# Low words of the float64 weights as a bit pattern from ScalarE, joined by one VectorE shift with xor

## The chip, the cores and the metric

The kernel runs on one core of one Trainium2 chip. The metric is the device time of one execution in microseconds (us), the median over runs. Engines are named as in the profile: PE (TensorE), PEld (its weight load), DVE (VectorE), ACT (ScalarE), POOL (GpSimd) and SP (SyncE, which issues most DMAs).

## The reference

Attention in which each query keeps its 32 best scores, and after it a feed-forward layer with a rational function. The feed-forward weights arrive as float64.

```
scores = scale * (q @ k.T)                       # 8 batches, 8 heads, 576 x 576, head_dim 64
kth    = the 32nd largest score of each row
attn   = softmax(where(scores >= kth, scores, -1e9))
x      = (attn @ v), heads side by side          # 4608 x 512
h      = x @ w_in                                # 512 x 2048
g      = (a0 + a1 h + a2 h^2 + a3 h^3) / (1 + |b0||h| + |b1| h^2 + 1e-6)
out    = g @ w_out                               # 2048 x 512
```

## The kernel before

**Attention.** Work goes by tiles of 128 queries of one head: 288 tiles. PE multiplies the scores of a tile into PSUM (`s`, line 583, one buffer of two banks), ACT copies them to `sb` (L590), DVE folds them and takes the best 32 (L609, L615, L626, L634), ACT takes `exp` (L688), DVE multiplies by the mask (L691), PE transposes the result (`trp`, L786), ACT copies that out (L798), and PE multiplies by the values (`av`, L812).

**Feed-forward.** 256 tokens make a chunk, which is complete after 16 tiles. A chunk runs in 8 groups of 256 hidden columns: `ph` (L953) on PE, five or six ACT and POOL steps, and `po` (L1113, L1120) on PE. A weight enters PE as a high part in `float32r` and a low part: `win_h`, `win_l`, and for half of `w_out` a high part in `wout` and a low part that goes to DRAM (`wout_l`) and comes back with each use.

**Weights.** There are 32 blocks of 128x512 (16 of `w_in`, 16 of `w_out`). `weight_block` loads a block's raw 64-bit words in two halves of 256 columns and makes float32 from the two 32-bit words `high` and `low` of each number. Per half: ACT writes the sign (L405); DVE shifts `high` left by three and turns the top bit into a PSUM tile `wb_w` (L412); a second DVE instruction shifts `low` right by 29 and ors it in (L420); ACT takes the absolute value of that (L426); POOL multiplies it by the sign (L430). A split block then gets a high part (L272 on ACT or L274 on POOL, 128x512) and a low part (POOL, L447).

**Order.** The order on every engine is fixed when the kernel is built: each step has a key, and `Plan.run` hands steps to the engines by key, assumed durations and free buffers. `KEY` holds the numbers. Buffers are rings: `t` has 9 tiles of 128x512 for weights and feed-forward, and `mm` has two PSUM banks, which `wb_w`, `trp`, `av` and `ph` share.

Of the kernel before, what the change touches and what calls it, by code (L numbers as in the profile page):

```python
# [12 lines left out]
I32 = mybir.dt.int32  # L13
BF16 = mybir.dt.bfloat16
# [5 lines left out]
KEY = {'LN': 12, 'UV': 'DVE', 'UK': -487.038, 'B0': ('ACT',), 'B1': ('POOL', 'DVE'), 'B2': ('DVE', 'POOL'), 'B3': ('DVE', 'POOL'), 'WH': ('ACT', 'POOL'), 'XH': ('POOL', 'ACT'), 'TH': 0, 'EU': -7.115, 'HW': 256, 'Q0': ('POOL', 'ACT'), 'Q1': ('POOL',), 'SPLIT': (0, 2, 4, 6), 'XS': 1, 'RH': ('ACT',), 'p2': ('POOL',), 'p4': ('POOL',), 'ratio': ('POOL',), 'ratio_low': ('POOL',), 'URG': -136.228, 'PT': -6.247, 'AV': -10.804, 'MOE': 55.899, 'LOOK': 0.277, 'T': 5.777, 'KL': 0.63, 'PJ': 40.462, 'WL': -6.889, 'EX': 42.775, 'EW': 13.493, 'ALT': {'ACT': 0.085, 'DVE': 78.296, 'POOL': 1.153}, 'WG': 0.783, 'QL': -3.371, 'PACE': 11.084, 'WI': 0, 'WO': 0, 'MS': -0.081, 'NM': ('POOL',), 'WD': ('POOL', 'ACT'), 'LP': ('POOL',), 'VL': -12.627}  # L20
# [157 lines left out]
def tile_topk_attention__then__rational_ffn(  # L178
# [10 lines left out]
    nc = tc.nc  # L189
# [19 lines left out]
    C1 = 1.0 + 1e-6  # L209
    HW = KEY['HW']  # L210
# [71 lines left out]
    def small(engs, long=0):  # L282
# [25 lines left out]
    nc.vector.tensor_scalar(far, far, 1.0 / 64.0, 1e-10, op0=ALU.mult, op1=ALU.add)  # L308
    tiny = const.tile([P, 1], F32, name="tiny")
    nc.gpsimd.memset(tiny, 1e-9)  # L310

    win_h = const.tile([P, HP, DFF], F32R, name="win_h")
    win_l = const.tile([P, HP, DFF], F32R, name="win_l")
    wout = [
        const.tile([P, DM], F32R if f // FG in SPLIT else F32, name=f"wout{f}") for f in range(NF)
    ]
# [12 lines left out]
    def weight_block(src, r0, e0, split, tags, key, nm, bits):  # L329
# [3 lines left out]
        steps = []  # L333
        hi, lo, away = split
        plain = lo is None and away is None
        hold = [Hold(n, 2 if plain and f64 else 1) for n in tags]
        xhold = Hold("mm", 2)

        def words(i, dtype=F32):
            n = hold[min(i, len(hold) - 1)]  # L340
            if n.tag != "xs":
                return buf(n, [P, 512], dtype, f"w_{nm}_{i}")
            if i % 2 == 0:
                o.big = buf(n, [P, HP, NT], dtype, f"w_{nm}_{i}", "hl"[i // 2])
                o.big = o.big.rearrange("p c n -> p (c n)")
            return o.big[:, (i % 2) * 512 : (i % 2 + 1) * 512]

        if not f64:

            def load():  # L350
                o.w = hi if plain else words(0)
                o.low = words(3 if f64 else 1, F32R) if away is not None else lo
                nc.sync.dma_start(o.w, rows)

            hold = [] if plain else hold[0 : 1 if away is None else 2]
            last = [add("SP", dma(1, P * 512), load, key=key, take=hold)]
        else:

            def load():
                o.raw, o.plain = [], []  # L360
                for i, e in enumerate(range(0, 512, 256)):
                    r = words(i).bitcast(I32)
                    nc.sync.dma_start(r, rows[:, e : e + 256].bitcast(I32))
                    o.plain.append(r.bitcast(F32)[:, 0:256])
                    r = r.rearrange("p (e t) -> p e t", t=2)
                    o.raw.append((slice(e, e + 256), r[:, :, 0], r[:, :, 1]))
                o.w = hi if plain else words(2)
                o.low = words(3, F32R) if away is not None else lo

            ld = add("SP", dma(2, P * 1024), load, key=key, take=hold)  # L370
            last, first = [], []
            for i in range(2):


                def upper(i=i):
                    es, low, high = o.raw[i]
                    nc.vector.tensor_scalar(
                        o.w[:, es].bitcast(I32), high, 3, 0x3FFFFFF8,
                        op0=ALU.logical_shift_left, op1=ALU.bitwise_and,
                    )  # L380

                def lower(i=i):
                    es, low, high = o.raw[i]
                    x = o.w[:, es].bitcast(I32)
# [4 lines left out]
                def ends(i=i):  # L389
                    es, low, high = o.raw[i]  # L390
                    x = o.w[:, es].bitcast(I32)
                    nc.vector.scalar_tensor_tensor(
                        x, high, -0x40000000, x, op0=ALU.bitwise_and, op1=ALU.bitwise_or
                    )

                if bits:
                    s1 = add("DVE", 0.38, upper, [ld], key + 1)
                    s2 = add("DVE", 0.5, lower, [s1], key + 1)
                    last.append(add("DVE", 0.5, ends, [s2], key + 2, give=hold if plain else []))
                    continue  # L400


                def sign(i=i):
                    es, low, high = o.raw[i]
                    nc.scalar.activation(o.w[:, es], high.bitcast(F32), AF.Sign)  # L405


                def high(i=i):
                    es, low, high = o.raw[i]
                    if i == 0:  # L410
                        o.bits = bank(xhold, [P, 512], f"wb_{nm}").bitcast(I32)
                    nc.vector.tensor_scalar(  # L412
                        o.bits[:, es], high, 3, 0x40000000,
                        op0=ALU.logical_shift_left, op1=ALU.bitwise_xor,
                    )

                def low(i=i):
                    es, low, high = o.raw[i]
                    x = o.bits[:, es]
                    nc.vector.scalar_tensor_tensor(  # L420
                        x, low, 29, x, op0=ALU.logical_shift_right, op1=ALU.bitwise_or
                    )

                def size(i=i):
                    es, low, high = o.raw[i]
                    nc.scalar.activation(o.plain[i], o.bits[:, es].bitcast(F32), AF.Abs)  # L426

                def join(i=i):
                    es, low, high = o.raw[i]
                    nc.gpsimd.tensor_tensor(  # L430
                        out=o.w[:, es], in0=o.plain[i], in1=o.w[:, es], op=ALU.mult
                    )

                s1 = add("ACT", act_sb(256), sign, [ld], key + 1)
                s2 = add("DVE", dve(256), high, [ld] + first, key + 1, take=[] if first else [xhold])
                first = [s2]
                s3 = add("DVE", dve(256), low, [s2], key + 1)
                s4 = add("ACT", act(256), size, [s1, s3], key + 2, give=[xhold])
                last.append(
                    add("POOL", pool_t(256), join, [s4], key + 2, give=hold if plain else [])  # L440
                )

        def high_part():
            affine(hi, o.w, 1.0, 0.0)

        def low_part():
            engine().tensor_tensor(out=o.low, in0=o.w, in1=hi.bitcast(F32), op=ALU.subtract)  # L447
# [8 lines left out]
        return [  # L456
            add("SP", dma(1, P * 512), lambda: nc.sync.dma_start(away, o.low.bitcast(F32)), [s],
                key + 3, give=hold)
        ]

    w_steps = {}

    def add_weights(key0, gap):
        n = 0
        blocks = []
        for e in range(0, DFF, 512):
            for c in range(HP):
                split = (win_h[:, c, e : e + 512], win_l[:, c, e : e + 512], None)
                tags = ["xs"] if c == HP - 1 and e < DFF // 2 else ["t"] * 3
                blocks.append((("i", c, e // 512), w_in, c * P, e, split, tags))  # L470
            for f in range(4 * (e // 512), 4 * (e // 512) + 4):
                split = (wout[f], None, wout_l.get(f))
                tags = ["t"] * (4 if f // FG in SPLIT else 2)
                blocks.append((("o", f), w_out, f * P, 0, split, tags))
        for n, (name, *args) in enumerate(blocks):
            bits = name[2] >= 4 - KEY["WI"] if name[0] == "i" else name[1] >= 16 - KEY["WO"]
            w_steps[name] = weight_block(*args, key0 + n * gap, f"w{n}", bits)
# [462 lines left out]
    def add_group(x, o, g, key, split, xs, oholds):  # L940
# [6 lines left out]
        def hidden(f, c):  # L947
            def emit():
                if f == 0 and c == 0:
                    y.ph = bank("mm", [P, 512], f"ph_{nm}")  # L950
                fs = slice((g * FG + f) * P, (g * FG + f + 1) * P)
                for i, (w, z) in enumerate(((win_h, o.xh), (win_h, o.xl), (win_l, o.xh))):
                    nc.tensor.matmul(  # L953
                        y.ph[:, f * NT : (f + 1) * NT], w[:, c, fs], z[:, c, :],
# [385 lines left out]
```

## Time and profile before

| what | value |
|---|---|
| median of 3 runs (lowest, highest) | 1576.05 us (1574.21, 1578.91) |
| the profiled execution's own time | 1577.03 us |
| its span, first to last instruction | 1574.9 us |
| mean granted TensorE clock | 0.967 of full |

2.1 us of the profiled execution lie outside its span. Busy time of an engine is the time in which it had an instruction; instructions of one engine overlap by some tenths of a microsecond, so means of single instructions add up to more than it.

### The profile page before, as it was taken

How to read it: one execution, taken by the hardware profiler on the slowest of the kernel's cores; microseconds unless marked ns; L12 is line 12 of the kernel's file. 1: busy time of each engine (PE TensorE's matmuls, PEld its weight loads, DVE VectorE, ACT ScalarE, POOL GpSimd, SP SyncE). 2: the span in 40 equal slices, each digit the busy share in tenths (PEclk: the TensorE clock that was granted, in tenths of full speed). 3: DMA queues.
4: the chain of work that ended last, by engine and by line, in shares of the span. 5: the costliest groups of instructions: out<-in, count | busy, mean ns of one | idle time of the engine just before them, and what ended most of it. 6: DMA issues, size and time to landing. Idle time of an engine off the chain costs nothing.

```text
span 1574.9 us, 31365 instructions
## 1 busy us (share of the span) xinstructions
PE 1436.9 (91%) x9441; PEld 1120.1 (71%) x9441; DVE 1415.8 (90%) x5605; ACT 1332.3 (85%) x2487; POOL 1144.2 (73%) x1601
## 2 busy tenths in 40 slices
PE   2346998988999899999999999999999999999996
PEld 1234776757777777777777877787787778788774
DVE  6998999999999999499999999999999999799742
ACT  5666897969898898899989998999897988798863
POOL 7767785758866796869867886678787896788520
PEclk9756999999999999999999999999999999999998
DMA  7544234122422233223432234224322333121111
GB/s 226 187 154 156 80 96 130 52 77 71 138 83 70 79 109 113 68 66 88 123 95 80 76 118 119 72 58 123 121 75 72 96 100 98 52 70 50 48 48 49
DMA packets 86802, 148.93 MB, mean 95 GB/s; under 512 B 12640, under 2 KB 38240, under 8 KB 86624
## 3 DMA queue, kind: packets, MB, share of 16 engines
q1 hardware_dynamic: 86560, 146.83, 31.4%
q8 instruction: 77, 1.26, 0.3%
q14 instruction: 101, 0.83, 0.2%
q0 software_dynamic: 64, 0.00, 0.1%
HBM read 134.22 MB, written 12.58 MB: 93 GB/s over the span
## 4 chain that ended last, share of the span: by engine, by line
PE 67%; POOL 8%; DVE 7%; ACT 6%; issue 2%; DMA 1%; POOLq 0%; ACTq 0%; DVEq 0%; SPq 0%
PE ph_m L953 18%; PE po_m L1113 11%; PE po_m L1120 9%; PE av L812 9%; PE s L583 7%; PE trp L786 6%; PE ph_t L953 3%; DVE m L626 2%; PE po_t L1113 1%; DVE pr L609 1%; PE s L580 1%; PE po_t L1120 1%; POOL pa_m L1041 1%; DVE pr L691 1%; ACT e L688 1%
## 5 line engine op out<-in xcount | busy, mean ns | idle before, releaser
L953 PE MATMUL ph_m<-xh_m,win_h 128*128 128x256 f32 x1024 | 316.4, 309 | 9.2 <-ACT p L798 8.8
L626 DVE MAX8 m<-x 128x8 f32<-128x192 f32 (+1 forms) x864 | 308.9, 358 | 3.6
L953 PE MATMUL ph_m<-xl_m,win_h 128*128 128x256 f32 x1024 | 289.5, 283 | 1.0 <-POOL xl_m L916 1.0
L953 PE MATMUL ph_m<-xh_m,win_l 128*128 128x256 f32 x1024 | 289.5, 283 | 0.0
L786 PE MATMUL trp<-ident,pr 128*128 128x128 f32 x1312 | 223.3, 281 | 45.0 <-DVE pr L691 24.3
L798 ACT COPY p<-trp 128x512 f32<-128x512 f32 (+1 forms) x448 | 230.2, 518 | 38.6 <-PE trp L786 25.4
L583 PE MATMUL s<-k,q 128*128 128x288 f32 x1024 | 209.5, 328 | 55.6 <-DVE x L609 36.4
L1113 PE MATMUL po_m<-wout,pa_m 128*128 128x512 f32 x512 | 248.2, 594 | 0.0
L786 PEld LDWEIGHTS trp<-ident,pr 128*128 128x128 f32 x1312 | 162.1, 144 | 109.2 <-issue 28.1
L609 DVE TENSOR_TENSOR pr<-s,sb 128x192 f32<-128x192 f32 x576 | 198.4, 346 | 41.7 <-PE trp L786 30.1
L688 ACT ACTIVATE e<-sb,st 128x576 f32<-128x576 f32 x288 | 218.7, 759 | 18.4 <-POOL st L280 11.5
L691 DVE SCALAR_TENSOR_TENSOR pr<-sb,m,e 128x576 f32<-128x576 f32 x288 | 230.3, 800 | 2.0 <-DVE x L615 0.2
L590 ACT COPY sb<-s 128x576 f32<-128x576 f32 x288 | 186.4, 647 | 51.8 <-PE s L583 45.0
L583 PEld LDWEIGHTS s<-k,q 128*128 128x128 f32 x1024 | 154.9, 196 | 98.3 <-ACT w_w L426 21.6
L953 PEld LDWEIGHTS ph_m<-xh_m,win_h 128*128 128x128 f32 x1024 | 195.2, 191 | 26.2 <-ACT p L798 13.9
L953 PEld LDWEIGHTS ph_m<-xl_m,win_h 128*128 128x128 f32 x1024 | 195.8, 191 | 8.3 <-issue 5.7
L615 DVE MAX8 x<-pr 128x8 f32<-128x192 f32 x576 | 199.1, 346 | 0.2
L634 DVE MATCH_REPLACE8 x<-m,x 128x192 f32<-128x192 f32 x576 | 198.0, 344 | 0.1
L953 PEld LDWEIGHTS ph_m<-xh_m,win_l 128*128 128x128 f32 x1024 | 195.1, 191 | 0.0
L812 PE MATMUL av<-p,vm 128*64 128x256 f32 (+1 forms) x1920 | 186.7, 343 | 2.6 <-ACT p L798 2.5
L812 PEld LDWEIGHTS av<-p,vm 128*64 128x64 f32 x1920 | 111.5, 142 | 82.9 <-issue 14.6
L975 POOL TENSOR_TENSOR pa_m<-pa_m,hh_m 128x512 f32<-128x512 f32 x88 | 113.2, 1286 | 38.6 <-ACT pa_m L972 38.0
(131 smaller groups left out, 3588.5 us busy)
## 6 DMA issues: line engine op xcount, KB each, us to landing
wl_m<-wout_l SPq DMA_DIRECT2D x128, 256.0 KB, 2.7
vm<-in_v_dram SPq DMA_DIRECT2D x96, 320.0 KB, 2.9
kx<-in_qk_dram SPq DMA_DIRECT2D x32, 576.0 KB, 3.9
qx<-in_qk_dram SPq DMA_DIRECT2D x64, 256.0 KB, 2.9
km<-in_qk_dram SPq DMA_DIRECT2D x32, 352.0 KB, 3.3
w_w<-in_moe_w_in_dram SPq DMA_DIRECT2D x32, 256.0 KB, 4.3
w_w<-in_moe_w_out_dram SPq DMA_DIRECT2D x32, 256.0 KB, 3.4
out_dram<-ob_m SPq DMA_DIRECT2D x64, 128.0 KB, 1.7
```

The costliest lines, as they stand in the source:

```text
L583: nc.tensor.matmul(s[:, hf, 0:HF], u.pair.q.q[:, i, t.h, o : o + P], kv.k[:, t.h, cols], start=(i == 0), stop=(i == 1),)
L609: engine().tensor_tensor(out=to, in0=one_, in1=two_, op=op)
L615: nc.vector.max(t.x[:, o : o + 8], t.w[:, 2 * i * TH :][:, 0:TH])
L626: nc.vector.max(t.m[:, 8 * r : 8 * r + 8], src)
L634: nc.vector.match_replace(y, t.m[:, 8 * r : 8 * r + 8], x, NEG)
L688: nc.scalar.activation(t.e, t.sb, AF.Exp, scale=SCALE, bias=t.st)
L691: nc.vector.scalar_tensor_tensor(out=t.pr, in0=t.sb, scalar=t.kth, in1=t.e, op0=ALU.is_ge, op1=ALU.mult, accum_out=u.ss[:, t.h : t.h + 1],)
L786: nc.tensor.transpose(u.ps[i][:, c * P : (c + 1) * P], u.pr[:, x], ident)
L798: nc.scalar.copy(pair.pT[i][:, at].rearrange("p c n -> p (c n)"), u.ps[i][:, 0 : n * P])
L812: nc.tensor.matmul(pair.av[d, 0 : u.nq * len(pair.units)], lhs, x[:, 0, d] if u.mixed else x[:, 0] if lone else x, start=(c == 0), stop=(c ...
L953: nc.tensor.matmul(y.ph[:, f * NT : (f + 1) * NT], w[:, c, fs], z[:, c, :], start=(c == 0 and i == 0), stop=(c == HP - 1 and i == 2),)
L1113: nc.tensor.matmul(o.po[i], y.pa[:, at], wout[ff], start=(ff == 0), stop=(ff == NF - 1),)
```

## The change

Per half block the work is divided anew. ACT reads `low` as an unsigned integer, multiplies it by 0.936 times two to the minus 51 and adds 2.0 (bias from a tile `two`); the float32 result has the bit pattern 0x40000000 with the wanted three bits at its end, and goes to PSUM. One DVE instruction shifts `high` left by three and xors it in. ACT then takes the sign of `high` in place, and the absolute value of the PSUM tile; POOL multiplies. `w_in` blocks load their raw words into the places of `win_h` and `win_l` (now 16 tiles each), so that only the float32 block takes a `t` tile; a `w_out` block takes two `t` tiles where a split one took four, its parts are made in them, and the high part is copied to `wout` by a further instruction (`high_again`). At most two `w_out` blocks are under way (`wt`).

Some 20 numbers in `KEY` change. The key step from one weight block to the next (`WG`) goes from 0.783 to 4.177, where a tile's step is 5.8 in both; the high parts may now go to POOL first (`WH`). `HW`, `SPLIT` and the shapes of all other instructions are as before.

```diff
@@ weight_block
-                def high(i=i):
-                    es, low, high = o.raw[i]
-                    if i == 0:
-                        o.bits = bank(xhold, [P, 512], f"wb_{nm}").bitcast(I32)
-                    nc.vector.tensor_scalar(
-                        o.bits[:, es], high, 3, 0x40000000,
-                        op0=ALU.logical_shift_left, op1=ALU.bitwise_xor,
-                    )
-
-                def low(i=i):
-                    es, low, high = o.raw[i]
-                    x = o.bits[:, es]
-                    nc.vector.scalar_tensor_tensor(
-                        x, low, 29, x, op0=ALU.logical_shift_right, op1=ALU.bitwise_or
-                    )
...
+                def low(i=i):
+                    es, low, high = o.parts[i]
+                    if i == 0:
+                        o.bits = bank(xhold, [P, 512], f"wb_{nm}")
+                        o.w = words(0) if lo is not None else hi if plain else hi(F32)
+                    nc.scalar.activation(o.bits[:, es], low.bitcast(U32), AF.Identity, scale=STEP, bias=two_)
+
+                def high(i=i):
+                    es, low, high = o.parts[i]
+                    x = o.bits[:, es].bitcast(I32)
+                    nc.vector.scalar_tensor_tensor(
+                        x, high, 3, x, op0=ALU.logical_shift_left, op1=ALU.bitwise_xor
+                    )
...
+                s1 = add("ACT", act(256), low, [ld] + first, key + 1,
+                         take=[] if first else [xhold] + (hold if lo is not None else []))
+                first = [s1]
+                s2 = add("DVE", dve(256), high, [s1], key + 1)
+                s3 = add("ACT", act_sb(256), sign, [s2], key + 1)
+                s4 = add("ACT", act(256), size, [s2], key + 2, give=[xhold])
                 last.append(
-                    add("POOL", pool_t(256), join, [s4], key + 2, give=hold if plain else [])
+                    add("POOL", pool_t(256), join, [s3, s4], key + 2, give=hold[i : i + 1] + turn[0 : i] if plain else [])
                 )
...
+        if f64:
+            steps.append(add(one(512, 0, KEY['WH']), None, high_again, [s], key + 3, give=hold[0:1]))
+        return steps
```

In the changed kernel the lines are: L390 `low`, L395 `high`, L401 `sign`, L405 `size`, L409 `join`, L274 or L276 the high parts, L431 the low part, L577 the copy to `sb`.

The first place is DVE between the best-of-eight steps of the first tile (`x`, `m`, `pr` are the tile's buffers, `wb_w` the bank of a weight block, `w_w` raw words). Before:

```order
L634 MATCH_REPLACE x_0_0_181<-m_0_0_201,x_0_0_181 128x192
L412 TENSOR_SCALAR wb_w_214<-w_w_0_144 128x256
L626 MAX m_0_0_201<-x_0_0_181 128x8
L420 SCALAR_TENSOR_TENSOR wb_w_214<-w_w_0_144,wb_w_214 128x256
L634 MATCH_REPLACE x_0_0_181<-m_0_0_201,x_0_0_181 128x192
L412 TENSOR_SCALAR wb_w_214<-w_w_1_146 128x256
L626 MAX m_0_0_201<-x_0_0_181 128x8
L420 SCALAR_TENSOR_TENSOR wb_w_214<-w_w_1_146,wb_w_214 128x256
```

The same place in the changed kernel:

```order
L621 MATCH_REPLACE x_0_0_174<-m_0_0_191,x_0_0_174 128x192
L395 SCALAR_TENSOR_TENSOR wb_w_194<-win_h_0_142,wb_w_194 128x256
L613 MAX m_0_0_191<-x_0_0_174 128x8
L596 TENSOR_TENSOR pr_0_0_173<-s_0_0_1_184,sb_0_0_1_200 128x192
L621 MATCH_REPLACE x_0_0_174<-m_0_0_191,x_0_0_174 128x192
L596 TENSOR_TENSOR pr_0_0_173<-s_0_0_1_184,sb_0_0_1_200 128x192
L596 TENSOR_TENSOR pr_0_0_173<-s_0_0_1_184,pr_0_0_173 128x192
L613 MAX m_0_0_191<-x_0_0_174 128x8
```

Where four weight instructions stood between the tile's steps, one stands now, and folds of the next tile have moved up.

The second place is the start of ACT. Before:

```order
L405 ACTIVATE w_w_2_132<-w_w_0_128 128x256
L405 ACTIVATE w_w_2_132<-w_w_1_130 128x256
L426 ACTIVATE w_w_0_128<-wb_w_150 128x256
L426 ACTIVATE w_w_1_130<-wb_w_150 128x256
L405 ACTIVATE w_w_2_140<-w_w_0_136 128x256
L405 ACTIVATE w_w_2_140<-w_w_1_138 128x256
L295 ACTIVATE co<-co 128x2
L590 COPY sb_0_0_0_174<-s_0_0_0_163 128x576
L426 ACTIVATE w_w_0_136<-wb_w_169 128x256
```

In the changed kernel, from the second weight block on:

```order
L390 ACTIVATE wb_w_156<-win_h_0_127,two 128x256
L390 ACTIVATE wb_w_156<-win_l_0_128,two 128x256
L577 COPY sb_0_0_0_162<-s_0_0_0_151 128x576
L401 ACTIVATE win_h_0_127<-win_h_0_127 128x256
L401 ACTIVATE win_l_0_128<-win_l_0_128 128x256
L405 ACTIVATE w_w_0_157<-wb_w_156 128x256 x2
L390 ACTIVATE wb_w_194<-win_h_0_142,two 128x256
L577 COPY sb_0_0_1_200<-s_0_0_1_184 128x576
L390 ACTIVATE wb_w_194<-win_l_0_143,two 128x256
```

ACT now opens a block's bank (L390) as well as closing it (L405), and the copies of score tiles stand inside that stretch; from its first to its last ACT instruction a block spans 3.4 rows of ACT before and 13.1 now, mean of the first 27 blocks.

The third place is ACT in the first feed-forward groups (`hh_m`, `pa_m`, `va_m`, `h_m`, `g_m` are the steps of a group). Before:

```order
L965 ACTIVATE hh_m_0_1_1751<-ph_m_0_1_1665 128x512
L272 ACTIVATE g_m_0_0_1758<-pa_m_0_0_1638 128x512
L798 COPY p_0_4_3_1762<-trp_0_4_3_1754 128x256
L972 ACTIVATE pa_m_0_1_1772<-ph_m_0_1_1665,co 128x512
L590 COPY sb_3_0_0_1780<-s_3_0_0_1764 128x576
L1023 ACTIVATE va_m_0_1_1790<-ph_m_0_1_1665 128x512
```

In the changed kernel, a few rows later in the same groups:

```order
L274 ACTIVATE g_m_0_0_1797<-pa_m_0_0_1605 128x512
L980 ACTIVATE va_m_0_1_1760<-va_m_0_1_1760,co 128x512
L390 ACTIVATE wb_w_1821<-w_w_0_1539,two 128x256
L577 COPY sb_3_0_1_1830<-s_3_0_1_1805 128x576
L390 ACTIVATE wb_w_1821<-w_w_1_1540,two 128x256
L274 ACTIVATE q_2_2_1843<-qx_2_2_1258 128x512
L401 ACTIVATE w_w_0_1539<-w_w_0_1539 128x256
L401 ACTIVATE w_w_1_1540<-w_w_1_1540 128x256
L405 ACTIVATE wout_1822<-wb_w_1821 128x256 x2
```

Before, no weight instruction stands behind the first group; now five of the 32 blocks do.

## Rows read from the trace of the kernel before

**Rows 1.** The page: span, busy time of the engines, PE and DVE in 40 slices.

```profile
span 1574.9 us, 31365 instructions
...
PE 1436.9 (91%) x9441; PEld 1120.1 (71%) x9441; DVE 1415.8 (90%) x5605; ACT 1332.3 (85%) x2487; POOL 1144.2 (73%) x1601
...
PE   2346998988999899999999999999999999999996
...
DVE  6998999999999999499999999999999999799742
```

**Rows 2.** Windows: start:end, length, busy us of each engine, granted PE clock, DMA.

```profile
core 0: us, PE busy (x) PEld busy (x) DVE busy (x) ACT busy (x) POOL busy (x), PEclk, DMA share, GB/s
12.00:154.00 142.00, 62.62 (x269) 42.00 (x270) 130.93 (x476) 98.21 (x228) 105.70 (x149) 0.74 0.56 177
154.00:256.00 102.00, 94.75 (x661) 73.91 (x661) 97.43 (x399) 83.13 (x152) 77.10 (x113) 0.97 0.37 110
256.00:1575.00 1319.00, 1279.54 (x8514) 1004.16 (x8512) 1187.06 (x4731) 1149.23 (x2106) 956.52 (x1327) 0.99 0.29 83
```

**Rows 3.** Waits from 12 to 154 us: total us, times, longest.

```profile
PE s L583 <- DVE x L609: 33.1, 10, 7.3
...
PE trp L786 <- DVE pr L691: 20.3, 9, 5.4
```

**Rows 4.** Timeline of PE at the first feed-forward matmul: start, duration, instruction.

```profile
152.94 1.96 PE L580 MATMUL s<-km 128*128 128x288 f32 x4
154.29 0.83 PE L953 MATMUL ph_m<-xh_m,win_h 128*128 128x256 f32 x1
```

**Rows 5.** Timeline of DVE among the weights of the first tile.

```profile
19.22 0.42 DVE L412 TENSOR_SCALAR wb_w<-w_w 128x256 int32<-128x256 int32 x1
19.55 0.35 DVE L626 MAX8 m<-x 128x8 f32<-128x192 f32 x1
```

**Rows 6.** Timeline of ACT in the same place.

```profile
20.21 0.75 ACT L405 ACTIVATE w_w<-w_w 128x256 f32<-128x256 f32 x2
20.86 0.62 ACT L272 ACTIVATE win_h<-w_w 128x512 fp32r<-128x512 f32 x1
21.39 0.37 ACT L426 ACTIVATE w_w<-wb_w 128x256 f32<-128x256 f32 x1
21.65 0.75 ACT L688 ACTIVATE e<-sb,st 128x576 f32<-128x576 f32 x1
22.31 0.38 ACT L426 ACTIVATE w_w<-wb_w 128x256 f32<-128x256 f32 x1
```

**Rows 7.** Groups by line and shape: count | busy us, mean ns | idle before.

```profile
L993 ACT ACTIVATE va_m<-va_m,co 128x512 f32<-128x512 f32 x128 | 94.5, 741 | 0.0
...
L1004 ACT ACTIVATE va_m<-va_m 128x512 f32<-128x512 f32 x128 | 82.6, 645 | 1.0
...
L430 POOL TENSOR_TENSOR w_w<-w_w,w_w 128x256 f32<-128x256 f32 x48 | 34.7, 729 | 18.2 <-ACT w_w L426 13.6 <-issue 2.7 <-POOL w_w L430 0.8
...
L412 DVE TENSOR_SCALAR wb_w<-w_w 128x256 int32<-128x256 int32 x64 | 26.7, 422 | 14.1 <-DMA w_w<-in_moe_w_in_dram 11.6 <-ACT x_m L829 0.8 <-ACT p L798 0.6
...
L274 POOL TENSOR_SCALAR q<-qx 128x512 fp32r<-128x512 f32 x36 | 22.3, 620 | 14.9 <-PE s L583 8.6 <-DMA qx<-in_qk_dram 6.1
L447 POOL TENSOR_TENSOR win_l<-w_w,win_h 128x512 fp32r<-128x512 f32 x16 | 20.4, 1273 | 4.1 <-ACT win_h L272 2.5 <-DMA kx<-in_qk_dram 1.4
...
L272 ACT ACTIVATE k<-kx 128x1152 fp32r<-128x1152 f32 x17 | 19.8, 1167 | 0.0
```

**Rows 8.** Timeline: two other users of an `mm` bank, from PE's start to ACT's copy.

```profile
24.37 1.09 PE L786 MATMUL trp<-ident,pr 128*128 128x128 f32 x4 [4.73 <-ACT wout L405]
...
25.49 0.58 ACT L798 COPY p<-trp 128x512 f32<-128x512 f32 x1 [0.30 <-PE trp L786]
...
53.73 4.24 PE L812 MATMUL av<-p,vm 128*64 128x256 f32 x20
...
58.02 0.37 ACT L829 COPY x_m<-av 128x256 f32<-128x256 f32 x1 [2.78 <-PE av L812]
```

**Rows 9.** Waits of DVE from 12 to 154 us.

```profile
DVE wb_w L420 <- ACT w_w L426: 5.7, 21, 0.6
```

More of the change, by code (lines that the diff above doesn't have):

```diff
@@ L13 @@
 I32 = mybir.dt.int32
+U32 = mybir.dt.uint32
 BF16 = mybir.dt.bfloat16
@@ L332, in weight_block @@
         f64 = rows.dtype != F32
-        steps = []
         hi, lo, away = split
         plain = lo is None and away is None
-        hold = [Hold(n, 2 if plain and f64 else 1) for n in tags]
-        xhold = Hold("mm", 2)
+        hold = [Hold("t") for _ in range(1 if lo is not None else 2)]
+        xhold, turn = Hold("mm", 2), [Hold("wt")]
         def words(i, dtype=F32):
[L340 to L346, printed above, removed]
+            return buf(hold[i], [P, 512], dtype, f"w_{nm}_{i}")
         if not f64:
@@ L351, in load @@
                 o.w = hi if plain else words(0)
[L352 removed]
+                o.low = words(1, F32R) if away is not None else lo if plain else lo()
+                o.hi = hi if plain else hi()
                 nc.sync.dma_start(o.w, rows)
[L355 removed]
+            hold = [] if plain else hold
             last = [add("SP", dma(1, P * 512), load, key=key, take=hold)]
@@ L359, in load @@
             def load():
-                o.raw, o.plain = [], []
+                to = [words(i) for i in range(2)] if lo is None else [hi(F32), lo(F32)]
+                o.parts = []
                 for i, e in enumerate(range(0, 512, 256)):
-                    r = words(i).bitcast(I32)
+                    r = to[i].bitcast(I32)
                     nc.sync.dma_start(r, rows[:, e : e + 256].bitcast(I32))
-                    o.plain.append(r.bitcast(F32)[:, 0:256])
                     r = r.rearrange("p (e t) -> p e t", t=2)
-                    o.raw.append((slice(e, e + 256), r[:, :, 0], r[:, :, 1]))
@@ new lines, in load, with sign, size, join @@
+                    o.parts.append((slice(e, e + 256), r[:, :, 0], r[:, :, 1]))
+            ld = add("SP", dma(2, P * 1024), load, key=key, take=hold + turn if lo is None else [])
+            last, first, final = [], [], []
+            for i in range(2):
+                def low(i=i):
[9 more added lines that the diff above has]
+                        x, high, 3, x, op0=ALU.logical_shift_left, op1=ALU.bitwise_xor
+                    )
+                def sign(i=i):
+                    es, low, high = o.parts[i]
+                    nc.scalar.activation(high.bitcast(F32), high.bitcast(F32), AF.Sign)
+                def size(i=i):
+                    es, low, high = o.parts[i]
+                    nc.scalar.activation(o.w[:, es], o.bits[:, es], AF.Abs)
+                def join(i=i):
+                    es, low, high = o.parts[i]
+                    nc.gpsimd.tensor_tensor(
+                        out=o.w[:, es], in0=o.w[:, es], in1=high.bitcast(F32), op=ALU.mult
+                    )
+                s1 = add("ACT", act(256), low, [ld] + first, key + 1,
[4 more added lines that the diff above has]
+                s4 = add("ACT", act(256), size, [s2], key + 2, give=[xhold])
@@ L439, in weight_block @@
                 last.append(
-                    add("POOL", pool_t(256), join, [s4], key + 2, give=hold if plain else [])
+                    add("POOL", pool_t(256), join, [s3, s4], key + 2, give=hold[i : i + 1] + turn[0 : i] if plain else [])
                 )
         def high_part():
-            affine(hi, o.w, 1.0, 0.0)
+            if lo is not None and f64:
+                o.hi, o.low = hi(), lo()
+            elif f64:
+                o.hi, o.low = words(0, F32R), words(1, F32R)
@@ L446, in low_part, with high_again @@
+            affine(o.hi, o.w, 1.0, 0.0)
         def low_part():
-            engine().tensor_tensor(out=o.low, in0=o.w, in1=hi.bitcast(F32), op=ALU.subtract)
+            engine().tensor_tensor(out=o.low, in0=o.w, in1=o.hi.bitcast(F32), op=ALU.subtract)
+        def high_again():
+            affine(hi(), o.hi.bitcast(F32), 1.0, 0.0)
         if plain:
```

91 lines of the change are left out of this document (31 added, 60 removed), and 2 rows, old and new, of the table room.

## Prediction

> **What bounds the kernel now.** The page comes first [rows 1]. PE is busy 91% of the span and DVE 90%, but in the 40 slices they are not bound at the same time: PE stands at 2 to 6 tenths in the first four slices (157 us) and at 9 nearly everywhere behind them, while DVE stands at 9 from the second slice on. So I cut the span into windows where that turns [rows 2]. From 12 to 154 us DVE is busy 130.9 of 142 us (92%), ACT 98.2, POOL 105.7, PE 62.6. From 154 to 256 us four engines are nearly full: DVE 97.4 of 102 (96%), PE 94.8, ACT 83.1, POOL 77.1. From 256 us on PE is the bound, 1279.5 of 1319 us (97%), and DVE has room (90%).
>
> The waits of the first window say what PE's idle time there is for [rows 3]: scores wait 33.1 us for DVE's folds (the `s` buffer is free only when DVE has read it), transposes 20.3 us for DVE's masked product. The window ends where the first `ph` matmul starts, at 154.29 us [rows 4]; in the order of both kernels 20 score tiles stand ahead of it. From there PE has as much work as it can do. Hence the yardstick: what the change is worth is by how much sooner PE gets through the first tiles, less what is given back in the next window. Behind 256 us the order on the engines differs little, and in the later two thirds hardly at all; PE, which is full there, has the same work, so a gain made before it is kept.
>
> **The change part by part.** An instruction that is taken out of a dense engine frees the distance from its start to the next one's, which is less than its duration. On DVE, L412 starts at 19.22 and the next at 19.55 [rows 5]: 0.33 us, where its mean alone is 0.422 [rows 7]. On ACT, two L405 start at 20.21 and what follows at 20.86, so 0.325 each; L272 0.53 (20.86 to 21.39); L426 0.26 (21.39 to 21.65) [rows 6].
>
> The new ACT instruction, `low`, is in no row: a strided read of 256 words, a pointer as bias, PSUM as its target. A pointer costs 0.096 (L993 at 741 ns has one, L1004 at 645 has none [rows 7]). With L405's 0.325 that is 0.42. From below L426 bounds it, 0.26, as if PSUM as target and the pointer cost nothing; from above L405's distance is replaced by its share of a pair that overlaps nothing, 0.75/2 plus pointer, and a little more for an integer source, 0.53. It reads the same words in the same step as L405, so I take 0.42. The DVE shift with xor has the form of L420 (strided words in, PSUM in and out) and I price it like L412, 0.33; both were there for each half and one stays.
>
> The order gives the counts up to the first `ph`. On DVE all 64 L412 go, and 54 of 64 joining instructions stand ahead of it (64 before): 74 by 0.33 is 24.4, so 130.9 falls to 106.5. On ACT: 53 `low` by 0.42 (+22.3); `sign` and `size` 52 each where 64 stood (-12 by 0.585, -7.0); copies of 512 columns 15 for 23 (-4.2); two splits of `k` fewer at 1.17 (-2.3), one more split of `x` (+0.6). 98.2 becomes 107.6. On POOL: 53 joins for 64 at 0.73 (-8.0), 21 low parts for 24 at 1.27 (-3.8), 11 high parts at 0.62 (+6.8), two `k` more and an `x` less at the like prices (+1.7): 105.7 becomes 102.4 [rows 2, 6, 7]. `high_again` is in these counts.
>
> So one engine at 131 becomes three at 102 to 108, and ACT leads narrowly. What share of the window can the busiest of three reach? DVE alone reached 92%; ACT reaches 81% in the next window, where four engines are full [rows 2]. ACT's weight work is filler that its queue can take whenever a half has landed, which is nearer to the first; I take 88%. 107.6/0.88 is 122 us, so the first `ph` starts at 12 + 122 = 134, 20 us sooner.
>
> In the next window the five blocks that are left (third place of the order) add to ACT 11 by 0.42, 12 by 0.585 and three copies, 13.2 us: 83.1 becomes 96.3; to DVE 10 by 0.33: 97.4 becomes 100.7. At DVE's own 96% the same work takes 105.4 us instead of 102 (+3.4); ACT at 88% would take 109.5 (+7.5). I take +5, between the two. Net: 20 - 5 = 15 us sooner at 256 us, and kept.
>
> The new wait is on ACT: `size` (and `sign`, which overwrites what DVE reads) waits for the xor on DVE. Behind it in ACT's queue stand copies of score tiles and `exp`; DVE's next folds wait for the former and the masked product for the latter. That is why 88% and not 92%.
>
> Priced at nothing: the loads. As many raw loads as before are issued on SP, the first block's in the same place of the queue, and the `w_in` blocks no longer wait for a `t` tile; the DMA engines are busy 56% in this window [rows 2]. If this cover went, a block would land later and only its own chain would move, which five blocks now do anyway.
>
> **Sum.** The profiled execution took 1577.0 us (span 1574.9 and 2.1 around it), 1 us above the median of the runs. 1577.0 - 15 = **1562.0 us**.
>
> **The range of the forecast itself.** At DVE's 92% and +3.4 the first `ph` comes at 129 and 22 us are kept: 1555. With `low` at 0.26 ACT falls to 99.0, and DVE, with 106.5, bounds: 1554. With `low` at 0.53 ACT is 113.3, at 88% 129 us, 13 sooner less 8: 1572. So 1554 to 1572.
>
> **Rivals.** *The work has only changed places.* ACT takes up more than DVE gives where both are in line: `low` costs 0.42, what it replaces 0.33. If ACT reaches only 78% with waits for DVE in its queue, the first window takes 107.6/0.78 = 138 us, 4 sooner, and the next gives 5 back: 1578, no change. For it: ACT's share was 69% there. Against it: it had no more to do there, and reached 81% where it had.
> The Trainium skill bears on this case: ScalarE: Activation LUTs, section Rules for kernel authors, sends additions and multiplications to VectorE, not ScalarE, since VectorE is faster per element. The trace agrees on the prices (0.42 against 0.33). Followed without looking at which engine is full, it would have the change cost time; the windows show the full one to be DVE.
>
> *The two banks of `mm` become the bound, and the time goes up.* A block held a bank from L412 at 19.22 to the end of its second L426 at 22.69, 3.5 us [rows 5, 6]; a transpose holds one 1.7 us (24.37 to 26.07), an `av` 4.7 us (53.73 to 58.39) [rows 8]. Up to the first `ph` that is 32 blocks, 27 transposes and 4 `av`: 112 + 46 + 19 = 177 of twice 142 us, 62%. Now ACT opens the bank and a block spans 13.1 rows of ACT. A row is 98.2/228 = 0.43 us [rows 2], so 5.6 us, at 88% 6.4; 27 blocks take 173, and with the rest 238 of twice 122 us: 98%. The order was made with these rings, so it can be run, but any delay on ACT now holds a bank that a transpose waits for. At 80% use the window takes 238/1.6 = 149 us: 7 later, 5 more in the next window: 1589. It costs more than no change from about 84% downwards. For it: the longer hold is in the order. Against it: the holds shrink with ACT's time, and transposes are not yet wanted by the feed-forward here.
> The two halves of a block lie in one bank, and DVE already waits for ACT between them, 21 times for 5.7 us [rows 9]. The Trainium skill, PSUM — Partial Sum Buffer, section PSUM bank collisions raise a hardware error, says why: two engines may not touch one bank in the same partitions at once, even in different columns. By it ACT's `low` of the second half and DVE's xor of the first can't overlap, which lengthens the hold and speaks for this rival; the trace agrees in that the wait is there.
>
> *More than forecast.* POOL and ACT keep up with the folds as DVE did, and the `t` tiles that weights no longer take let the first groups run closer: below 1554.
>
> **Chances.** Forecast 0.58; below 1554 0.06; work only moved (1572 to 1581) 0.18; banks, or another queue that stalls (above 1581), 0.18. A measurement here tells 0.3% (4.7 us) from no change. Faster: the first two, 0.64; same 0.18; slower 0.18. The range takes in the case of no change and the nearer part of the bank case: 1552 to 1586.
>
> **What the profile will show.** Right: from 12 us to the first `ph` DVE busy near 106, ACT near 107, POOL near 102; the first `ph` between 129 and 138 us; `low` at 0.45 to 0.53 us alone; no change behind 256 us but a shift. Wrong: the first `ph` behind 145 us with PE's transposes waiting for ACT's L405 (banks), or ACT with gaps that DVE's L395 ended (work moved); or a first `ph` that comes early and a window behind it in which PE waits for low parts of `w_in` (L431), which would mean that the blocks were put off too far.

## The result, and the profile after

The changed kernel takes **1558.49 us** (median of 4 runs, 1557.28 to 1559.08); the kernel before took 1576.1 us beside it. The ratio is 0.9886, with a 95% interval of 0.9869 to 0.9903: 17.6 us, or 1.1%, sooner. The forecast was 1562 us, in a range of 1552 to 1586.

The page of the changed kernel, with the same lines as [rows 1] (the last one is ACT's 40 slices):

```profile
span 1556.3 us, 31312 instructions
...
PE 1431.3 (92%) x9441; PEld 1115.2 (72%) x9441; DVE 1391.3 (89%) x5541; ACT 1351.4 (87%) x2542; POOL 1155.5 (74%) x1619
...
PE   2447899999999999999999999999999999999996
...
DVE  6888999999999899499999999999999989799742
ACT  6888997989898898899999998999897988798873
```

The span is 18.6 us shorter. PE's part of that can be read here: span less busy time was 138.0 us before and is 125.0 now, so of the 18.6 us 13.0 are idle time and 5.6 are busy time. The work of PE is the same 9441 matmuls. The mean granted clock went from 0.967 to 0.971 of the full 2.4 GHz: of PE's busy time 54.2 us lay in stretches at 1.2 GHz before and 51.6 now. That difference is worth some 1.3 us (an estimate: half of it, at twice the clock). What took away the other 4 us of busy time is not shown.

The first `ph` matmul (PE's timeline, as [rows 4]) now starts at 139.11 us, 15.2 us sooner:

```profile
139.11 0.39 PE L940 MATMUL ph_m<-xh_m,win_h 128*128 128x256 f32 x1 [0.89 <-ACT p L785]
```

The windows of [rows 2], cut at the same points of the work (first `ph`; first group of the second chunk):

```profile
12.00:139.00 127.00, 60.78 (x272) 39.37 (x272) 108.73 (x415) 106.60 (x256) 102.37 (x149) 0.76 0.56 184
139.00:249.00 110.00, 97.44 (x645) 73.47 (x646) 101.42 (x407) 95.34 (x186) 87.96 (x126) 0.94 0.38 116
249.00:1556.00 1307.00, 1273.10 (x8526) 1002.36 (x8524) 1180.95 (x4721) 1147.16 (x2100) 959.11 (x1331) 0.99 0.29 84
```

One engine at 131 of 142 us has become three at 109, 107 and 102 of 127 us: DVE 86%, ACT 84%, POOL 81%. PE does the same work in the first window (60.8 us against 62.6) in 15 us less.

What waits there now, 12 to 139 us (as [rows 3] and [rows 9]: total us, times, longest):

```profile
PE trp L773 <- ACT wout L405: 15.8, 5, 3.8
DVE wb_w L395 <- ACT wb_w L390: 15.7, 8, 11.8
...
PE trp L773 <- ACT w_w L405: 12.8, 4, 4.1
PE s L570 <- DVE x L596: 12.3, 6, 3.1
```

PE's waits for DVE's folds are down from 33.1 to 12.3 us, and the 20.3 us for the masked product are no longer among the long ones. In their place transposes wait 28.6 us for ACT's `size`, the instruction that closes a weight block's bank. Before, they waited 8.8 us for ACT's weight instructions:

```profile
PE trp L786 <- ACT wout L405: 8.8, 2, 4.7
```

Of DVE's 15.7 us for `low`, 11.8 are one wait at the start of the program.

The new instructions (groups by line and shape: count | busy us, mean ns of one | idle before):

```profile
L390 ACT ACTIVATE wb_w<-w_w,two 128x256 f32<-128x256 uint32 x32 | 15.8, 501 | 0.4 <-ACT va_m L980 0.2
L401 ACT ACTIVATE w_w<-w_w 128x256 f32<-128x256 f32 x32 | 13.9, 437 | 0.2
L395 DVE SCALAR_TENSOR_TENSOR wb_w<-w_w,wb_w 128x256 int32<-128x256 int32 x32 | 13.6, 426 | 7.8 <-ACT wb_w L390 5.5 <-ACT wout L405 2.0
```

ACT's timeline through one block of `w_out`, and behind it DVE's two instructions for this block, which show how its bank is held:

```profile
27.50 0.49 ACT L390 ACTIVATE wb_w<-w_w,two 128x256 f32<-128x256 uint32 x1
27.94 0.63 ACT L577 COPY sb<-s 128x576 f32<-128x576 f32 x1
28.47 0.48 ACT L390 ACTIVATE wb_w<-w_w,two 128x256 f32<-128x256 uint32 x1
28.88 1.15 ACT L274 ACTIVATE k<-kx 128x1152 fp32r<-128x1152 f32 x1
...
36.59 0.38 ACT L405 ACTIVATE wout<-wb_w 128x256 f32<-128x256 f32 x1
```

```profile
33.99 0.42 DVE L395 SCALAR_TENSOR_TENSOR wb_w<-w_w,wb_w 128x256 int32<-128x256 int32 x1
...
34.59 0.41 DVE L395 SCALAR_TENSOR_TENSOR wb_w<-w_w,wb_w 128x256 int32<-128x256 int32 x1
```

`low` opens the bank at 27.50, and `size` closes it at 36.97: 9.5 us. A score copy stands between the two `low`, but most of the time is a wait for DVE: the second `low` ends at 28.95, and DVE, busy with the tiles' best-of-eight steps, comes to the first xor at 33.99. From the first `low` to the end of the second `size`, the 26 blocks that are closed ahead of the first `ph` hold a bank 6.4 us on average (3.1 to 12.1): 1.6 us to the end of the second `low`, 2.9 from there to the end of the second xor on DVE, 1.9 to the end of the second `size`. Before, it was 3.4 us over 32 blocks.

### The profile page after: what moved, and what is told of

Same layout as the page of the kernel before. It is cut to its first block, busy times and chain, and to the rows that moved or that the text cites. A ratio compares the mean times of both kernels' runs of the same rounds, so it can differ in the third digit from the quotient of the medians.

```text
span 1556.3 us, 31312 instructions
## 1 busy us (share of the span) xinstructions
PE 1431.3 (92%) x9441; PEld 1115.2 (72%) x9441; DVE 1391.3 (89%) x5541; ACT 1351.4 (87%) x2542; POOL 1155.5 (74%) x1619
## 4 chain that ended last, share of the span: by engine, by line
PE 75%; ACT 9%; DVE 6%; POOL 4%; DMA 3%; issue 2%; SPq 1%; POOLq 0%; ACTq 0%; DVEq 0%
PE ph_m L940 20%; PE po_m L1100 12%; PE po_m L1107 11%; PE av L799 10%; PE trp L773 8%; PE s L570 7%; PE ph_t L940 3%; PE s L567 2%; ACT p L785 2%; PE po_t L1100 1%; DVE m L613 1%; PE po_t L1107 1%; ACT sb L577 1%; ACT e L675 1%; DMA out_dram<-ob_m 1%
## 5 line engine op out<-in xcount | busy, mean ns | idle before, releaser
L785 ACT COPY p<-trp 128x512 f32<-128x512 f32 (+1 forms) x448 | 231.2, 520 | 28.6 <-PE trp L773 20.1
L577 ACT COPY sb<-s 128x576 f32<-128x576 f32 x288 | 186.5, 647 | 50.7 <-PE s L570 37.0
L962 POOL TENSOR_TENSOR pa_m<-pa_m,hh_m 128x512 f32<-128x512 f32 x88 | 113.2, 1287 | 34.5 <-ACT pa_m L959 33.6
```

The lines of the kernel that those rows point to most:

```text
L577: nc.scalar.copy(t.sb, t.s[:, :, 0:HF])
L785: nc.scalar.copy(pair.pT[i][:, at].rearrange("p c n -> p (c n)"), u.ps[i][:, 0 : n * P])
```

## The experiments

**The theory.** The gain is DVE's relief in the first 250 us, and ACT and POOL now bound that stretch together with DVE. **Rivals:** the retuned numbers of `KEY` made the gain (`WG` above all); the new places for raw words made it; and the prediction's bank rival, that the two `mm` banks now cost time. All times are medians; each run stands beside runs of the kernel before on the same chip (1576.2 to 1577.4 us), and ratios are to those. "First `ph`" is from the timeline of PE. The changed kernel is at 1558.5 us and 139.1 us.

| run | us | ratio to before, 95% | first `ph`, us |
|---|---|---|---|
| extra_dve | 1579.5 | 1.0018 (1.0009 to 1.0027) | 156.7 |
| low_twice | 1588.4 | 1.0070 (1.0053 to 1.0086) | 163.8 |
| no_sign | 1553.4 | 0.9855 (0.9840 to 0.9871) | 136.8 |
| no_xor | 1553.1 | 0.9850 (0.9837 to 0.9864) | 138.0 |
| two_dve | 1584.8 | 1.0048 (1.0035 to 1.0061) | 148.2 |
| key_before | 1587.4 | 1.0066 (1.0053 to 1.0079) | 169.7 |
| two_dve_kb | 1587.5 | 1.0080 (1.0066 to 1.0094) | 168.2 |
| wg_back | 1580.7 | 1.0034 (1.0022 to 1.0046) | 166.4 |
| kb_wg4 | 1572.7 | 0.9980 (0.9971 to 0.9990) | 142.5 |
| before_wg | 1590.8 | 1.0090 (1.0073 to 1.0107) | 151.5 |
| bank_o20 | 1574.6 | 0.9990 (0.9981 to 0.9999) | 144.0 |
| bank_o27 | 1607.5 | 1.0189 (1.0175 to 1.0203) | 131.7 |

### Load put on and taken off, in an unchanged order

In the first four runs the instructions stand in the order of the changed kernel; only one kind is added or left out.

**extra_dve**: one more DVE instruction per half (it stands ahead of the shift with xor, not behind it as the expectation says).

```diff
 def high(i=i):
...
+    nc.vector.tensor_scalar(
+        x, x, 0, 0, op0=ALU.logical_shift_left, op1=ALU.bitwise_xor,
+    )
     nc.vector.scalar_tensor_tensor(
         x, high, 3, x, op0=ALU.logical_shift_left, op1=ALU.bitwise_xor
     )
```

> The changed kernel in its own order, with one more VectorE instruction of 128x256 on the bank behind each shift with xor (64 in all, 54 of them before the first ph; it shifts by nothing and leaves the numbers as they are). Theory (three engines are nearly equally the bound in the first 139 us): the cost of 54 by 0.33 = 18 us comes back nearly whole: 1568 to 1578 us. Rival (ScalarE or the mm banks are the bound now and VectorE has room): at most 5 us more, 1558 to 1563 us.

**low_twice**: `low` issued twice.

```diff
+    nc.scalar.activation(o.bits[:, es], low.bitcast(U32), AF.Identity, scale=STEP, bias=two_)
     nc.scalar.activation(o.bits[:, es], low.bitcast(U32), AF.Identity, scale=STEP, bias=two_)
```

> The changed kernel in its own order, with ScalarE's low issued twice for each half (64 more, 53 of them before the first ph). Theory (ScalarE is one of three that bound the first window): 53 by 0.42 = 22 us more on ScalarE, whose busy time there goes from 110 to 132 us; 1574 to 1584 us, first ph at 153 to 163 us. Rival (VectorE alone still is the bound and ScalarE fills its idle time): at most 5 us more, 1558 to 1563 us.

The windows from 12 us to the first `ph`, of extra_dve:

```profile
12.00:157.00 145.00, 64.35 (x273) 41.20 (x274) 130.81 (x469) 108.65 (x257) 104.08 (x150) 0.75 0.49 162
```

and of low_twice:

```profile
12.00:164.00 152.00, 62.80 (x273) 40.19 (x274) 108.96 (x418) 132.76 (x311) 103.66 (x149) 0.72 0.48 157
```

Both times are a little above what was expected, by 1.5 and 4 us. With extra_dve DVE is back at 130.8 us, its load before [rows 2], and the first `ph` (156.7 against 154.3 us) and the time (1579.5 against 1576.9 us) are back near before, though ACT's `low`, the places and the order are all new. That is the theory's main evidence: 22.1 us more on DVE move the first `ph` by 17.6 us and the end by 21.0. But 26.2 us more on ACT do as much: 24.7 and 29.9 us. Either engine, loaded more, sets the window's length. Both edits also lengthen a block's chain, though, and with it the hold of its bank, from 6.5 us (mean of the first 27 blocks) to 7.5 and 7.9 us; the transposes' wait for `size` grows from 28.6 to 34.5 and 37.6 us. So what comes from the load and what from the bank is not told apart here. The times lie above the ranges at least in part for the price: the added instructions cost more than was reckoned (last section).

**no_sign**: the 64 `sign` instructions left out; **no_xor**: the 64 `high` instructions left out, each by a `return` ahead of the instruction.

> The changed kernel in its own order without the 64 sign instructions on ScalarE (the join then multiplies by the raw word instead of a sign, so that the weights are wrong; as many instructions on the other engines). 53 by 0.33 = 17 us less on ScalarE before the first ph. Theory (VectorE, ScalarE and POOL bound the first window together, so relief of one shows little): 2 to 8 us sooner, 1550 to 1556 us. Rival (ScalarE or the banks that its row of instructions holds lead clearly): 12 to 20 us sooner, 1538 to 1546 us. Other rival (VectorE leads): no change.

> The changed kernel in its own order without the 64 VectorE instructions that shift and xor (the weights then lack their upper words; all else runs as before). 54 by 0.33 = 18 us less on VectorE before the first ph, and one step less in each block's chain. Theory (VectorE, ScalarE and POOL bound the first window together): as with the sign left out, a small part of it, 2 to 8 us sooner: 1550 to 1556 us. Rival (VectorE leads, since 64 more instructions on it cost 21 us): 12 to 20 us sooner, 1538 to 1546 us.

The same window of no_sign:

```profile
12.00:137.00 125.00, 62.76 (x273) 40.06 (x274) 109.19 (x415) 91.62 (x205) 104.17 (x150) 0.80 0.56 187
```

and of no_xor:

```profile
12.00:138.00 126.00, 60.24 (x272) 39.27 (x272) 93.83 (x362) 105.84 (x258) 103.97 (x150) 0.76 0.56 185
```

15.0 us less on ACT bring 5.1 us at the end, 14.9 us less on DVE bring 5.4, and the first `ph` moves by 2.3 and 1.1 us. As the theory had it: what is added to one of the equally full engines shows about whole (95% and 114%), what is taken from one shows by a third. Neither DVE nor ACT leads. That POOL bounds the window with them, as the theory says, no run tried. no_sign bears on the banks, too: the transposes' wait for `size` falls from 28.6 to 18.7 us in an unchanged order, and the first `ph` comes only 2.3 us sooner:

```profile
PE trp L773 <- ACT wout L405: 12.0, 5, 3.1
...
PE trp L773 <- ACT w_w L405: 6.7, 3, 2.5
```

### Arithmetic, ordering numbers and places

In these runs the order is planned anew for each kernel.

**two_dve**: the old arithmetic in the new places, with the new numbers.

```diff
-    nc.scalar.activation(o.bits[:, es], low.bitcast(U32), AF.Identity, scale=STEP, bias=two_)
+    nc.vector.tensor_scalar(
+        o.bits[:, es].bitcast(I32), high, 3, 0x40000000,
+        op0=ALU.logical_shift_left, op1=ALU.bitwise_xor,
+    )
...
-        x, high, 3, x, op0=ALU.logical_shift_left, op1=ALU.bitwise_xor
+        x, low, 29, x, op0=ALU.logical_shift_right, op1=ALU.bitwise_or
...
-    s1 = add("ACT", act(256), low, [ld] + first, key + 1,
+    s1 = add("DVE", dve(256), low, [ld] + first, key + 1,
```

> The changed kernel with its places for raw words and its ordering numbers, but with the arithmetic of before: both joining instructions of a half on VectorE again (shift and xor, then shift and or), ScalarE's low left out. The order is planned anew. Theory (the gain is VectorE's relief in the first 250 us): VectorE gets 54 instructions back before the first ph, 54 by 0.33 us = 18 us, so its busy time there rises from 111 to 129 us, the first ph starts at 150 to 156 us where the changed kernel has 139, and the time is 1570 to 1578 us. Rival (the new ordering numbers, or the places in win_h and win_l and the freed t tiles, made the gain): first ph near 139 us and 1555 to 1561 us.

**key_before**: the changed kernel with before's line `KEY`. **two_dve_kb**: both edits, so that only the places are new, with what hangs on them (the copy `high_again`, at most two `w_out` blocks under way, the sign behind the joining instructions).

> The changed kernel with the ordering numbers of before; arithmetic and places stay new. Theory (VectorE's relief): most of the gain stays, 1556 to 1567 us, with a first ph that is a little later or earlier than 139 us since the weights are urgent again (WG 0.783), up to 32 blocks ahead of it. Rival (the numbers made the gain): 1573 to 1580 us.

> The changed kernel's places for raw words alone: old arithmetic (two VectorE instructions a half, no low on ScalarE) and all ordering numbers of before. Theory (the places gain nothing by themselves; with weights urgent and nothing of t to hold them back, attention starts late): 1575 to 1600 us. Rival (the places are what made room and the old arithmetic suits the old numbers): 1556 to 1570 us.

With the changed kernel these make a square (all in the new places):

| | numbers of before | new numbers |
|---|---|---|
| two DVE instructions a half | 1587.5 us | 1584.8 us |
| ACT's `low` and one DVE instruction | 1587.4 us | 1558.5 us |

The theory as it was stated for key_before is wrong: with the old numbers the new arithmetic gains nothing. So is the rival as stated: with the old arithmetic the new numbers gain 3 us, less than the 0.3% that a measurement here can tell. Only together do they gain 29. two_dve missed its theory's range as well: its first `ph`, at 148.2 us, came sooner than the 150 to 156 us expected, and 6 us sooner than before, but the end came at 1584.8 us, 7 us behind the range; nothing of the early start is left. And the places, with what hangs on them, cost 11 us against before (1587.5 to 1576.2). What goes wrong with the old numbers is seen in the window from 40 to 80 us, most of all in key_before:

```profile
40.00:80.00 40.00, 0.17 (x1) 0.20 (x2) 15.97 (x45) 38.58 (x101) 34.21 (x41) 1.00 0.67 214
```

and in its longest wait of PE in that window:

```profile
PE trp L773 <- DVE pr L678: 45.7, 1, 45.7
```

ACT is full with weights (38.6 of 40 us), PE is idle, DVE is busy 16.0 us, and attention waits. In two_dve_kb, without `low` on ACT, PE works 7.3 us there and POOL is the fullest (36.7). Before, a `w_in` block needed three tiles of the ring `t` (all but two of the blocks), and `t` with its nine tiles could hold the blocks back (argued from the code: no run takes this apart); with raw words in places of their own `w_in` blocks are held by little but their keys, and with `WG` at 0.783 those are urgent. Two runs try `WG` by itself.

**wg_back**: one number of the changed kernel. **kb_wg4**: the numbers of before with the same number new.

```diff
-'WG': 4.177
+'WG': 0.783
```

> The changed kernel with one number put back: the key step between weight blocks, WG, from 4.177 to 0.783. Theory (with raw words of w_in loaded into their own places the ring t no longer holds weight blocks back, so of the retuned numbers it is WG that must spread them): nearly all of what the old numbers cost (1587.4 against 1558.5 us) comes back from this number alone, 1577 to 1592 us, with ACT full and PE idle between 40 and 80 us. Rival (the other numbers matter as much, or any step off the tuned point costs some 10 us): 1560 to 1572 us.

> The changed kernel with all ordering numbers of before except WG, which stays at 4.177. Theory (WG alone of the numbers matters): 1556 to 1568 us, within 10 us of the changed kernel. Rival (the numbers work together): 1570 to 1590 us.

The window from 40 to 80 us of wg_back:

```profile
40.00:80.00 40.00, 3.61 (x14) 2.58 (x14) 17.39 (x50) 37.95 (x97) 34.25 (x45) 1.00 0.62 200
```

and of kb_wg4:

```profile
40.00:80.00 40.00, 15.25 (x68) 10.38 (x70) 33.08 (x124) 36.27 (x87) 34.37 (x49) 0.69 0.66 222
```

`WG` alone takes 22.2 of the 28.9 us away and gives 14.7 of them back: it is most of the numbers' worth, not all (kb_wg4 is 5 us above what the theory allowed; the numbers work together). With it PE works 15 us in this window (14.2 before), without it 4.

**before_wg**: is it then the spreading that gains, whatever the arithmetic? The kernel before with `WG` at 3.5. (The new 4.177 has no order with its buffers; the other new numbers were not tried in it.)

> The kernel before with one number changed: the key step between weight blocks, WG, from 0.783 to 3.5 (of the new 4.177, which its buffers don't allow); arithmetic and places are old. Rival (spreading the weight blocks is the gain, whatever the arithmetic): 1556 to 1566 us. Theory (the numbers pay only with the new arithmetic, where ScalarE must carry a third instruction per half between attention's steps; with two VectorE instructions a half VectorE stays the one that is full, wherever the blocks lie): no gain, 1572 to 1592 us.

13 us slower. The first `ph` comes 2.8 us sooner than before, but then PE has 80.0 busy us from 151 to 256, where it has 96.3 in the kernel before:

```profile
151.00:256.00 105.00, 80.00 (x509) 60.68 (x508) 88.38 (x340) 78.07 (x147) 68.90 (x93) 0.89 0.31 97
```

Why is not shown: ten of the 64 halves are made there, but PE's longest waits are for ACT's copies of transposes (7.5 us) and for `size` (4.2), and no wait for a high or low part is among them. This step of 3.5 by itself is no gain with the old arithmetic and places.

### The banks

**bank_o20** and **bank_o27**: the bank of the first 20 or 27 blocks from the ring `o`.

```diff
-        xhold, turn = Hold("mm", 2), [Hold("wt")]
+        xhold, turn = Hold("o" if int(nm[1:]) < 20 else "mm", 2), [Hold("wt")]
```

> The changed kernel, with the bank in which a weight block is put together taken from the ring o in place of mm for the first 20 blocks (o has two banks that only the feed-forward's second product uses, from about 145 us on). The order is planned anew. Rival of the prediction (the two banks of mm cost time: transposes wait 28.6 us for ScalarE's size in the first window): 4 to 12 us sooner, 1546 to 1555 us. Theory (the engines are the bound and the bank waits mostly lie where they would wait anyway): within 4 us of the changed kernel, or slower by the price of a plan that was not tuned for it, 1555 to 1575 us.

> As bank_o20, but for the first 27 blocks, all that stand ahead of the first ph. Rival of the prediction (banks): 1544 to 1555 us. Theory (engines): 1555 to 1578 us.

PE's waits from 12 to 139 us of bank_o20:

```profile
PE s L570 <- DVE x L596: 21.0, 9, 3.8
PE trp L773 <- DVE pr L678: 16.2, 8, 8.1
...
PE trp L773 <- ACT wout L405: 4.5, 1, 4.5
```

The waits for ACT's `size` fall from 28.6 to 4.5 us, and waits for DVE take their place (37.2 us, where the changed kernel has 12.3 for the folds). bank_o27 does reach its first `ph` 7.4 us sooner, but with only 48 `size` ahead of it where the changed kernel has 53, so not all of that need be the banks; and it ends 49 us later, 30 us behind what even the theory allowed. The feed-forward's second product shares `o` with the weights there; that this is the reason was not shown. Both runs have a new order for which no numbers were tuned, so the price of the banks in the order of the changed kernel stays open between nothing and some 7 us; no_sign (10 us less of these waits, 2.3 us gained) speaks for the lower end. No kernel tried that computes the right output is faster than the changed one.

## Why the prediction was right

- **What bounds the window, and the loads.** Forecast to the first `ph`: DVE 106.5, ACT 107.6, POOL 102.4 us. Measured from 12 us: 108.7, 106.6, 102.4. The counts from the order times the distances between starts gave the loads to 2%. `low` was forecast at 0.45 to 0.53 us alone, from [rows 6, 7], and takes 0.50.
- **The share that is mis-sized.** The forecast let the busiest engine fill 88% of the window: 122 us, first `ph` at 134. ACT filled 84% (106.6/127) and DVE 86%: first `ph` at 139.1, 15.2 us sooner in place of 20. This term was 5 us off. The runs fit this reading: with one engine clearly ahead, the share is 90% (extra_dve, 130.8/145) or 87% (low_twice, 132.8/152), and DVE's was 92% before; with three alike, each also waits for the others. 88% was a share for one leader, and there was none. The two kinds lie close (84 to 86% and 87 to 92%), so this is a reading and not a proof. It puts the first `ph` 1 us behind the 129 to 138 us that the prediction gave as a sign.
- **The new wait.** It was put on ACT, for the xor. In the trace it stands on PE: transposes wait 28.6 us for the `size` that frees the bank. That was the bank rival's mechanism, and its hold was forecast at 6.4 us and measured at 6.4. The reason was reckoned from the rows of ACT between `low` and `size`; the trace shows DVE in it, too: of the 6.4 us, 2.9 go by until DVE has done both xors, so a part of these waits is still DVE's full queue. In no block does `low` of the second half overlap the xor of the first, as the prediction had it. With the other users as measured now (transposes 38 us, `av` 18, from PE's start to the end of ACT's copy) and 169 us for the weights, the two banks are used 225 of 254 us, 89% where the rival reckoned 98%. Its point of decision, 84%, was passed on the good side. That this margin is worth time by itself is not shown.
- **What the next window gives back, and what came behind it.** The sum was "20 - 5 = 15 us sooner at 256 us, and kept". Read by PE's idle time, since the groups stand in another order and the matmuls done by 256 us differ: up to the first `ph` PE was idle 13.1 us less than before; of this 5.3 were given back up to the first group of the second chunk (252.1 us before, 249.1 now), which is the 5 of the forecast; 7.8 were left. Up to group 19 (372.9 us before, 357.7 now) 3.8 more came, and with it matmuls at the higher clock; at this point both kernels have done the same 1614 matmuls, and the last of the groups (the 128th) starts 17.2 us sooner. So the step that failed is that behind 256 us there is "no change but a shift", and with it "PE is the bound" from there on: up to 373 us the kernel before still waited. At 256 us the forecast was 15 us, and 7.8 us of PE's idle time were saved there. That the total came out within 4 us is luck in part: a gain of some 7 us behind that point, which was not forecast, stands in for the 7 us that were missing at it.

The two windows, of the kernel before:

```profile
252.00:373.00 121.00, 108.88 (x732) 84.91 (x730) 115.45 (x474) 100.38 (x184) 74.78 (x116) 0.96 0.24 68
```

and of the changed kernel:

```profile
249.00:358.00 109.00, 100.60 (x701) 79.84 (x700) 108.15 (x450) 97.23 (x177) 74.70 (x115) 1.00 0.25 72
```

PE is idle 12.1 us there before and 8.4 now, and the granted clock is 0.96 before and 1.00 now, which over 121 us is worth up to 0.04 x 121 = 4.8 us (an estimate): together they cover it. In the window ahead of it the clock went the other way, 0.97 before [rows 2] and 0.94 now.

- **The loads on the DMA queues** were priced at nothing. The DMA share of the first window is 0.56 as before, and no transfer stands among the long waits shown. But the places were not free: with the old numbers, they and what hangs on them cost 11 us (that the brake of the ring `t` is what is missing was argued above, not shown). The prediction had this only inside the counts of the new order and gave it no price of its own.
- **The rivals.** *Only moved* would have shown ACT at 78%; it came to 84%. It is what happens with the old numbers (1587.4 for 1587.5 us). The rule of the Trainium skill, ScalarE: Activation LUTs, section Rules for kernel authors, that sends element-wise additions and multiplications to VectorE, would have kept the work where it was; here the result goes against it, since DVE was the full engine and ACT had room. On the price alone the trace agrees: one `low` takes ACT 0.50 us, and the instruction that it replaces took DVE 0.42 [rows 7]. *More than forecast* (below 1554 us) did not come, with the first window at 127 us and not shorter than the 122 forecast.

What stays open: whether the kernel before, with the new arithmetic in its old places and numbers set for it, would gain as much, and which of the some 20 numbers besides `WG` matter (neither was tried); and what the banks cost.

## What to carry to other kernels

When one engine is full and others are not, work can move to a dearer engine with profit, but look for the point at which they are equally full: here 26 us more on ACT then cost 30. For the window, take a little less than a single leader's share (here 84 to 86% against 87 to 92%). When a change gives work new places and a new division, set the order anew before judging it: with the old numbers the same arithmetic gained nothing. A milestone such as the first feed-forward matmul is half a yardstick: three re-planned kernels reached it sooner than the one they came from, or than the kernel before, and ended later; read PE's idle time and clock at a point where the two orders have met.

## What the runs showed of the hardware

In two of the runs an instruction reads or overwrites what the one just before it on the same engine wrote, and the program has it wait for a semaphore that the first one raises. In the trace it starts only when the first has ended. DVE in extra_dve, start and duration:

```profile
12.13 0.43 DVE L395 TENSOR_SCALAR wb_w<-wb_w 128x256 int32<-128x256 int32 x1 [12.13 <-ACT wb_w L390]
12.59 0.43 DVE L398 SCALAR_TENSOR_TENSOR wb_w<-win_h,wb_w 128x256 int32<-128x256 int32 x1
```

and ACT in low_twice, where both write the same words:

```profile
12.14 0.49 ACT L390 ACTIVATE wb_w<-win_l,two 128x256 f32<-128x256 uint32 x1
12.67 0.49 ACT L391 ACTIVATE wb_w<-win_l,two 128x256 f32<-128x256 uint32 x1
13.09 0.19 ACT L297 ACTIVATE co<-co 128x2 f32<-128x2 f32 x1
```

The two of a pair start 0.46 and 0.53 us apart (the means over all 64 pairs are 0.46 and 0.52), where an instruction that needs nothing of its neighbour follows after 0.42 (12.67 to 13.09; on DVE 0.33, [rows 5]). So an added instruction cost 0.41 us of busy time on DVE (22.1 us for 54) and 0.49 on ACT (26.2 for 53), not 0.33 and 0.42 as was expected of these two runs. The prediction's prices, taken from instructions that stand between others, gave the changed kernel's loads to 2%.
